# Attention scores as 64-column fp32 products in their own half of the PSUM partitions

## The chip, the core and the metric

The kernel runs on one core of a Trainium2 chip. The time is device time in microseconds (us) of one execution, given as a median of runs. TensorE (PE in the profile) multiplies a stationary operand, the weights, with a moving operand and writes to PSUM. VectorE is DVE, ScalarE is ACT, GpSimd is POOL, and SyncE (SP) issues the transfers.

## The reference, cut to what matters

The input is q, k, v of shape (8 batches, 8 heads, 576, 64) and p of shape (8, 8, 32, 64). Two attention steps come first, then two layers of products that do not matter for this change.

```python
def sm_attn(qq, kk, vv):
    s = scale * np.matmul(qq, kk.transpose(0, 1, 3, 2))
    s = s - np.max(s, axis=-1, keepdims=True)
    a = np.exp(s)
    a = a / (np.sum(a, axis=-1, keepdims=True) + 1e-09)
    return np.matmul(a, vv)
p_packed = sm_attn(p, k, v)               # 32 queries per head against 576 keys
out = sm_attn(q, p_packed, p_packed)      # 576 queries per head against 32 keys
...
h = max(x @ w1, x @ w2, x @ w3); x = h @ w_out        # 512 -> 768 -> 512
h = x @ w_in; x = (h * cos(h)) @ w_out                # 512 -> 2048 -> 512
```

## The kernel before

**Units.** The attention work is cut into 16 units, one for each batch `b` and each group `g` of four heads (two head pairs). A raw tile holds one head pair: 128 partitions are the 64 dimensions of two heads, 576 columns are the positions. A unit has two such tiles of k and two of q.

**The two score products of a unit.** `S1` multiplies the packed queries p with k, and `S2` multiplies the packed keys that step one has produced with q. Both call `scores(w, x)` (line 491; the matmul is at line 495). The weights `w` have shape 128 x 2 x 128: for each head pair `pi` there are 128 weight columns. Only 64 of them are filled, 32 for each of the two heads of the pair; the other 64 are zeros, cleared once at the start. In `pz` (step one) pair 0 fills columns 0 to 63 and pair 1 fills columns 64 to 127 (`pdst`, line 437). In `bt` (step two) it is the same for even batches, and the other way round for odd ones (`Ba`, line 608). The moving operand is one half `hf` of the 576 columns, 288 wide. For each half the two pairs are added up in one PSUM region of 128 partitions x 288 (`start` on the first, `stop` on the second); the zeros make the sum a mere placing of each pair in its own 64 partitions. So a unit has two score products of four matmul calls each, 32 products in all. Both operands are plain fp32, and the trace has two weight loads and two matmul instructions for each such call; nearly all other matmuls of the kernel are split by hand into float32r parts with one instruction for each call.

**What reads the scores.** The tile `big` is a PSUM tile of two banks. After `S1` DVE takes the maximum (`S1m`, line 508) and ACT the exponentials (`E1`, line 523); then come transposes (`Tp`, line 535), the product with v (`Pp`, line 560, or line 702 for the first two batches) and the transpose `Bp` (line 602), from which ACT and DVE fill `bt` and `wt` (lines 610, 613, 616). After `S2` DVE transposes the scores in blocks (`S2t`, line 629).

**The order.** Each engine works through a list that is fixed when the program is built. For the first two and the last two batches a planner (`Order`) sorts the steps by the costs in its table (2.1 for `S1` and `S2`); for the others `att_pos` places them by hand between the products of the first layer: `zps` (line 739, folding weights), `h` (line 818) and `x` (line 848). The diff changes neither the table nor the places, so every engine has its steps in the same order. After the attention, from about 505 us on, the second layer follows (lines 1363, 1794, 1832), in which there are no score products.

**Row halves in the kernel before.** For the first two batches line 702 ends each product with v in a matmul whose operands have only 64 rows. The trace shows it as `64*128`, beside `128*128` for the rest.

## Time and profile before

| | us |
|---|---|
| median of 3 runs | 1352.8 (1352.47 to 1353.12) |
| profiled execution | 1350.07 |
| its span, first to last instruction | 1348.3 |
| PE busy | 1313.1 (97%) |
| DVE, ACT, POOL busy | 898.2, 713.7, 363.1 |
| mean granted clock of TensorE | 0.995 |

The span is what the trace covers, and the profiled execution's own time is 1.8 us above it. Busy times are unions of instructions, so they say how much of the span an engine had something under way. Matmuls are pipelined: a matmul's duration is longer than the distance from its start to the next one's start, and it is this distance that counts when many follow each other.

### The profile page before, as it was taken

The page shows a single profiled execution, that of the slowest core. Times are in us where ns is not written, and L with a number is a line of the kernel's source. Part 1 is how long each engine was busy: PE and PEld are TensorE (multiplying, and loading weights), DVE is VectorE, ACT ScalarE, POOL GpSimd, SP SyncE. Part 2 cuts the span into 40 slices and gives each one's busy share as a digit, 9 for nine tenths or more (in the row PEclk, how much of TensorE's full clock was granted, in tenths as well). Part 3 has the DMA queues.
Part 4 walks back from the last instruction along what each step waited for, and adds up shares of the span by engine and source line. Part 5 has one row for each costly group of instructions (what it writes and reads, how often), then busy time and mean ns, then how long its engine had stood idle before and what let it go on. Part 6 is the DMA issues. An engine that isn't in the chain of part 4 may idle for free.

```text
span 1348.3 us, 22165 instructions
## 1 busy us (share of the span) xinstructions
PE 1313.1 (97%) x8130; PEld 1187.2 (88%) x8130; DVE 898.2 (67%) x1511; ACT 713.7 (53%) x1413; POOL 363.1 (27%) x340
## 2 busy tenths in 40 slices
PE   7889999999999998999999999999999999999998
PEld 5679999899989998888888899999999999999997
DVE  6885565546554677898578797666666566665655
ACT  4564435142513245555355576657666666666754
POOL 7572113030303006772013023203232032420300
PEclk9899999999999999999999999999999999999999
DMA  9777468445844478657021475756657566575630
GB/s 341 235 217 205 158 177 232 147 160 166 227 152 163 122 232 317 233 162 279 1 94 63 156 235 164 239 182 199 217 175 245 174 210 206 184 237 179 217 128 32
DMA packets 108140, 251.54 MB, mean 187 GB/s; under 512 B 17408, under 2 KB 40960, under 8 KB 108032
## 3 DMA queue, kind: packets, MB, share of 16 engines
q1 hardware_dynamic: 108032, 250.13, 57.9%
q8 instruction: 64, 1.05, 0.3%
q14 instruction: 44, 0.36, 0.1%
HBM read 180.88 MB, written 52.43 MB: 173 GB/s over the span
## 4 chain that ended last, share of the span: by engine, by line
PE 87%; DVE 7%; DMA 2%; ACT 2%; issue 2%; SPq 0%; POOL 0%; ACTq 0%; DVEq 0%; POOLq 0%
PE po L1832 26%; PE g L1794 21%; PE h L818 12%; PE x L848 9%; PE g L1363 6%; PE big L495 4%; PE zps L739 3%; PE po L1468 3%; DMA zd<-zx 1%; DVE m L833 1%; PE big L560 1%; PE big L702 1%; PE big L535 1%; DVE pv L577 1%; DVE wm L1575 0%
## 5 line engine op out<-in xcount | busy, mean ns | idle before, releaser
L1832 PE MATMUL po<-w,gh 128*128 128x512 f32 x1560 | 392.6, 389 | 0.0
L1832 PEld LDWEIGHTS po<-w,gh 128*128 128x128 f32 x1560 | 277.3, 188 | 43.9
L1794 PEld LDWEIGHTS g<-xc,wr 128*128 128x128 f32 x2160 | 284.2, 189 | 16.3
L1794 PE MATMUL g<-xc,wr 128*128 128x256 f32 x2160 | 288.4, 281 | 0.0
L818 PE MATMUL h<-at,z 128*128 128x256 f32 (+1 forms) x1728 | 249.6, 300 | 6.0 <-DMA z<-zx 3.0
L818 PEld LDWEIGHTS h<-at,z 128*128 128x128 f32 x1728 | 234.1, 191 | 12.8 <-DVE m L833 4.4
L1316 POOL TENSOR_TENSOR xc<-xr,xc 128x256 fp32r<-128x256 f32 x95 | 90.9, 977 | 498.0 <-ACT xc L1312 475.2
L1402 ACT ACTIVATE y<-y 128x512 f32<-128x512 f32 x144 | 91.0, 632 | 151.6 <-DVE y L1398 151.6
L848 PE MATMUL x<-hh,w 128*128 128x320 f32 (+1 forms) x1152 | 159.4, 296 | 4.6 <-DVE hh L303 1.6
L848 PEld LDWEIGHTS x<-hh,w 128*128 128x128 f32 x1152 | 154.7, 188 | 8.6 <-DVE hh L303 2.4
L1426 DVE TENSOR_TENSOR gh<-y,gh 128x512 fp32r<-128x512 f32 x144 | 109.0, 757 | 51.0 <-ACT gh L1422 50.9
L1406 DVE TENSOR_TENSOR y<-y,hs 128x512 f32<-128x512 f32 x112 | 84.2, 752 | 74.3 <-ACT y L1402 74.1
L1817 DVE TENSOR_TENSOR hs<-mc,g 128x256 f32<-128x256 f32 x168 | 70.0, 418 | 71.9 <-PE g L1794 69.9
L1422 ACT CAST gh<-y 128x512 fp32r<-128x512 f32 x144 | 88.8, 617 | 32.5 <-DVE y L1406 32.4
L1392 DVE SCALAR_TENSOR_TENSOR y<-y 128x512 f32<-128x512 f32 x128 | 93.9, 734 | 16.8 <-ACT y L1384 16.3
L833 DVE TENSOR_TENSOR m<-m,h 128x576 f32<-128x576 f32 x96 | 72.2, 752 | 48.2 <-PE h L818 27.2
L320 POOL TENSOR_SCALAR w<-wraw 128x512 fp32r<-128x512 f32 x56 | 88.9, 1598 | 28.3 <-DMA wraw<-w_in 10.2
L1805 ACT COPY mc<-g 128x256 f32<-128x256 f32 x168 | 62.3, 371 | 58.0 <-PE g L1794 57.4
L1363 PE MATMUL g<-x,w 128*128 128x512 f32 x384 | 92.0, 389 | 0.0
L756 DVE TENSOR_TENSOR zx<-zps,zx 128x512 fp32r<-128x512 f32 (+1 forms) x80 | 50.5, 635 | 57.8 <-ACT zx L751 53.6
L1363 PEld LDWEIGHTS g<-x,w 128*128 128x128 f32 x384 | 72.0, 188 | 14.9
L751 ACT CAST zx<-zps 128x512 fp32r<-128x512 f32 (+1 forms) x80 | 43.2, 542 | 74.5 <-PE zps L739 28.9
(120 smaller groups left out, 1575.8 us busy)
## 6 DMA issues: line engine op xcount, KB each, us to landing
wr<-sd SPq DMA_DIRECT2D x152, 512.0 KB, 3.5
zd<-zx SPq DMA_DIRECT2D x64, 256.0 KB, 3.6
z<-zd SPq DMA_DIRECT2D x32, 512.0 KB, 4.6
z<-zx SPq DMA_DIRECT2D x56, 256.0 KB, 3.2
wr<-sd SPq DMA_DIRECT2D x56, 256.0 KB, 3.2
sd<-w SPq DMA_DIRECT2D x24, 512.0 KB, 3.4
wraw<-w_out SPq DMA_DIRECT2D x22, 512.0 KB, 4.6
wraw<-w SPq DMA_DIRECT2D x18, 512.0 KB, 6.4
```

The lines of the kernel that those rows point to most:

```text
L320: nc.gpsimd.tensor_scalar(out=w[:, 1, :], in0=hi32.bitcast(F32), scalar1=0.0, scalar2=None, op0=ALU.mult)
L818: nc.tensor.matmul(ps[:, T0 + c0:T0 + c0 + nt], zt[b, j, g][:, x, c:c + P], at[b, g][:, y, c0:c0 + nt], start=(n == 0), stop=(n == 3 * NG ...
L833: nc.vector.tensor_tensor(out=m, in0=m, in1=ps[:, T0:T0 + S], op=ALU.max)
L848: nc.tensor.matmul(ps[:, T0 + c0:T0 + c0 + nt], w[:, x, d * P:(d + 1) * P], hh[f][:, y, c0:c0 + nt], start=(n == 0), stop=(n == 3 * NF - 1),)
L1316: EITHER[eng].tensor_tensor(out=x[:, 1, kk, :], in0=x_part(t, *XSRC[i], kk), in1=x[:, 0, kk, :].bitcast(F32), op=ALU.subtract)
L1363: nc.tensor.matmul(ps, w[:, a, kc * P:(kc + 1) * P], x2[t, kc][:, b, :], start=(n == 0), stop=(n == 3 * KC - 1),)
L1392: nc.vector.scalar_tensor_tensor(out=y, in0=r, scalar=MAGIC, in1=y, op0=ALU.subtract, op1=ALU.subtract)
L1402: nc.scalar.activation(out=r, in_=y, func=AF.Sin, scale=TWO_PI if c < NF2 else -TWO_PI)
L1422: nc.scalar.copy(g[:, 0, :], gs[c])
L1426: nc.vector.tensor_tensor(out=g[:, 1, :], in0=gs.pop(c), in1=g[:, 0, :].bitcast(F32), op=ALU.subtract)
L1794: nc.tensor.matmul(ps, w[:, a, c:c + P], x[:, b, kk, :], start=(i < 3 and n == 0), stop=(n == 5), skip_group_check=True,)
L1832: nc.tensor.matmul(po[t][s], g[:, a, s * P:(s + 1) * P], w[:, b, :], start=(f == 0 and i == 0), stop=(f == NF2 - 1 and i == 2),)
```

## The change

`scores` no longer adds two products of 128 weight columns into 128 PSUM partitions. Each pair multiplies only its 64 filled weight columns and writes its own 64 partitions, each matmul call being a group of its own. `swap` says which half belongs to which pair; step two passes the parity of the batch. The number of calls stays four for each product, with the same 288 moving columns, in the same order: for each half `hf`, first pair 0 and then pair 1.

```diff
-            def scores(self, w, x):
+            def scores(self, w, x, swap=0):
                 ps = self.big()
                 for hf in range(2):
                     for pi in range(2):
+                        c = (pi ^ swap) * D
                         nc.tensor.matmul(
-                            ps[:, hf, :HS], w[:, pi, :], x[pi][:, hf * HS:(hf + 1) * HS], start=(pi == 0), stop=(pi == 1)
+                            ps[c:c + D, hf, :HS], w[:, pi, c:c + D], x[pi][:, hf * HS:(hf + 1) * HS], start=True, stop=True
                         )
                 return ps[:, :, :HS]
...
             def S2(self):
-                self.s2 = self.scores(self.bt, self.qr)
+                self.s2 = self.scores(self.bt, self.qr, self.b % 2)
```

## Rows read from the trace of the kernel before

**Rows 1.** The page: busy time of the engines, and the chain that ended last.
```profile
PE 1313.1 (97%) x8130; PEld 1187.2 (88%) x8130; DVE 898.2 (67%) x1511; ACT 713.7 (53%) x1413; POOL 363.1 (27%) x340
...
PE 87%; DVE 7%; DMA 2%; ACT 2%; issue 2%; SPq 0%; POOL 0%; ACTq 0%; DVEq 0%; POOLq 0%
```

**Rows 2.** Busy time by stretch, all instructions: PE, PEld, DVE, ACT, POOL, clock, DMA.
```profile
0.00:100.00 100.00, 81.13 (x396) 65.07 (x397) 81.52 (x146) 54.36 (x105) 66.57 (x69) 0.95 0.81 267
100.00:505.00 405.00, 398.76 (x2721) 374.26 (x2721) 231.61 (x410) 144.44 (x290) 74.54 (x70) 1.00 0.60 178
505.00:1349.00 844.00, 833.23 (x5016) 747.86 (x5015) 585.04 (x956) 514.90 (x1019) 221.98 (x201) 1.00 0.55 181
```

**Rows 3.** Busy time by stretch of line 495 alone: PE, PEld, clock, DMA.
```profile
0.00:100.00 100.00, 22.27 (x64) 14.64 (x64) 0.95 0.81 267
100.00:505.00 405.00, 51.20 (x192) 35.46 (x192) 1.00 0.60 178
```

**Rows 4.** The chain, 100 to 505 us and 0 to 100 us: line 495's pieces.
```profile
by line: PE h L818 32.4%; PE x L848 26.4%; PE big L495 11.0%; PE zps L739 9.2%; PE big L560 3.5%; DVE m L833 2.3%; DVE pv L577 1.7%; issue 1.6%; PE big L535 1.5%; DMA zd<-zx 1.3%; DVE ms L637 1.0%; DVE e L641 1.0%; ACT e L651 0.8%; DVE hh L
...
221.16 1.94 PE big L495 x8
...
6.50 4.19 PE big L495 x8
13.97 3.15 PE big L495 x8
35.81 1.95 PE big L495 x8
42.47 4.21 PE big L495 x8
```

**Rows 5.** Line 495: durations in ns, least, median, most.
```profile
L495 PE MATMUL big<-raw,pz x128: 403/406/849, 6.5 to 422.9; 128*128 128x288 f32 x128
L495 PEld LDWEIGHTS big<-raw,bt x128: 186/190/193, 24.3 to 500.4; 128*128 128x128 f32 x128
L495 PE MATMUL big<-raw,bt x128: 403/406/510, 24.3 to 500.7; 128*128 128x288 f32 x128
```

**Rows 6.** Timeline, 220.6 to 223.5 us, PE and its weight loads: start, us.
```profile
220.77 1.88 PEld L495 LDWEIGHTS big<-raw,pz 128*128 128x128 f32 x8
221.00 2.10 PE L495 MATMUL big<-raw,pz 128*128 128x288 f32 x8
```

**Rows 7.** Timeline of weight loads around the 64-row matmuls of line 702.
```profile
50.42 0.84 PEld L702 LDWEIGHTS big<-raw,at 128*128 128x128 f32 x4
...
57.48 1.59 PEld L702 LDWEIGHTS big<-raw,at 128*128 128x128 f32 x8 [1.06 <-DVE at L694]
59.40 0.29 PEld L702 LDWEIGHTS big<-raw,at 64*128 64x128 f32 x2 [0.33 <-issue]
60.03 0.53 PEld L739 LDWEIGHTS zps<-w,wt 128*128 128x128 f32 x3 [0.33 <-issue]
```

**Rows 8.** Timeline of PE, 0 to 75 us: first and later score products.
```profile
6.50 4.18 PE L495 MATMUL big<-raw,pz 128*128 128x288 f32 x8 [2.66 <-DMA pz<-pT]
12.64 1.33 PE L535 MATMUL big<-ident,e 128*128 128x128 f32 x5 [1.97 <-ACT e L523]
13.84 3.27 PE L495 MATMUL big<-raw,pz 128*128 128x288 f32 x8
...
35.65 2.10 PE L495 MATMUL big<-raw,pz 128*128 128x288 f32 x8
39.71 1.13 PE L535 MATMUL big<-ident,e 128*128 128x128 f32 x5 [1.96 <-ACT e L523]
42.47 4.21 PE L495 MATMUL big<-raw,pz 128*128 128x288 f32 x8 [1.63 <-DVE at L694]
```

**Rows 9.** Waits of PE, 100 to 505 us: us in total, times, longest.
```profile
PE big L495 <- DVE wt L616: 1.5, 4, 0.4
PE big L495 <- DVE at L549: 0.3, 1, 0.3
```

**Rows 10.** Timeline of PE, 100 to 505 us: a score product after such a wait.
```profile
240.81 2.21 PE L495 MATMUL big<-raw,bt 128*128 128x288 f32 x8 [0.38 <-DVE wt L616]
```

## Prediction

> **What bounds the kernel now.** I read the page first. PE has work under way for 97% of the span, and 87% of the chain that ended last is PE [rows 1]. Busy time alone says little of a pipelined engine, so the stretches come next. From 100 to 505 us PE is busy for 398.8 of 405 us, and DVE for 231.6, ACT for 144.4, with the DMA engines at 0.60 [rows 2]: there PE sets the pace. Before 100 us PE is busy for 81.1 of 100 and DVE for 81.5; nobody is full, and the end is set by a chain through several engines. After 505 us line 495 has no instruction, so the change can only shift that part as a whole.

> Where is line 495? It has 64 matmul instructions before 100 us and 192 after, so at eight to a product there are 8 products early and 24 in the stretch that PE bounds [rows 3]. The chain of 100 to 505 us has 11.0% of its time on line 495 [rows 4], which is 44.6 us; 24 products of 1.94 us would be 46.6, so nearly every microsecond of these products is on the path. Of the early eight the chain names four, together 13.5 us [rows 4].

> **What one product costs now.** Eight instructions cover 2.10 us [rows 6], the last of them 0.406 by its own duration [rows 5], so starts lie (2.10 - 0.41) / 7 = 0.242 us apart: a slot. Eight slots are 1.94 us, which is also the chain's piece [rows 4]. The weight loads cover 1.88 us and begin 0.23 us ahead of the matmuls [rows 6]: each is hidden behind the matmul before it. So cutting a load from 128 to 64 columns gains nothing by itself here; the slot is that of the 288 moving columns, and the diff leaves their number, and that of the instructions, as it is.

> **What the change can give.** What changes is that two pairs no longer use the same part of the array's columns, nor the same PSUM partitions. If matmuls on different halves may run at the same time, the order of issue decides how much. In order they are A, A, B, B, A, A, B, B (two fp32 instructions for each call). [...] Then the slots are: A; A with B; B with A; A with B; B. Five slots in place of eight, 1.21 us, a gain of 3 x 0.242 = 0.73 us. If halves do not overlap, the gain is nothing. No row of before has two halves side by side: the only narrow matmuls, those of 64 rows, come in pairs on the same half [rows 7]. These are the two bounds, 0 and 0.73. I take 0.73: the operands, weight cells and results of A and B are disjoint after the change, and what the rows show of this engine is that it does start work that has its own place ahead of time, as the loads do [rows 6].

> [...]

> **What it costs.** The price is that of entering and leaving the narrow form. Line 702 pays it before the change, with 64 rows in place of 64 columns. Loads in a run of 256-column fp32 matmuls are (0.84 - 0.19) / 3 = 0.217 apart, 0.19 being one load's own time [rows 7]. From the first 64-row load at 59.40 to the first load after, at 60.03, there is 0.63 us for two matmuls, of which 0.43 would be their slots: 0.20 us more [rows 7]. The way in is the same: eight loads from 57.48 to 59.40 are 1.92 us. The loads stand still for 0.33 us on either side [rows 7]. The 0.20 has two parts. The two 64-row loads cover 0.29 us, so the second starts 0.29 - 0.19 = 0.10 after the first: the first load is not hidden, 0.10. The other 0.10 is the array running empty. A product surrounded by full-width work pays on both sides: on leaving 0.20, since the next load has 128 columns; on entering 0.10 of emptying and a load of 64 columns, between 0.05 (half of the 128-column load, an estimate) and 0.10. I take 0.15. Together 0.35, up to 0.40.

> [...]

> Between the halves there are three places where a load for the other half may come too late to be hidden, if loads are taken only one ahead of the matmuls. The bounds for that are 0 and 3 x 0.10 = 0.31 us; with loads half as long 0.16. Nothing of before shows loads more than one ahead, and nothing excludes it; I take 0.08, the middle of 0 and 0.16.

> **The sum.** From 100 to 505 us: 0.73 - 0.35 - 0.08 = 0.30 us for each of 24 products, 7.2 us. Five of them follow an idle PE, of 0.30 to 0.38 us [rows 9, 10]. The emptying falls into that wait, and the load after it stood bare before too (2.21 us against 2.10 [rows 10, 6]) and gets shorter. So entering changes these five from a cost of 0.15 to a gain of 0.05: 5 x 0.2 = 1.0 us more. The wait itself is for ACT and DVE work on a transpose that PE has just done, and moves with PE. Behind a product in PE's queue stand `h`, `zps` or `x`, which have their operands: the waits of PE on line 495 are 1.8 us of the 405 [rows 9]. So I count these 8.2 us in full.

> Before 100 us the products on the chain are four [rows 4, 8]. At 6.50 and 42.47 the slot is about 0.48, twice the other ((4.21 - 0.85) / 7, the longest record taken off [rows 5, 8]): 3 x 0.48 = 1.4 us each. Both follow a wait, so entering is free; the first also ends in a wait of 1.97, the other pays 0.2 for leaving. At 13.84 the mean slot is 0.41: 1.2 less 0.4 for both sides. At 35.65 it is 0.73 less 0.15, with a wait of 1.96 behind it. That makes 1.4 + 1.2 + 0.8 + 0.6 = 4.0. DVE is as busy as PE here, and DVE and DMA hold the chain between these pieces, so something else will end some of these waits: between 0 and 4.0, I take half, 2.0.

> Total: 8.2 + 2.0 = 10.2 us. The profiled execution would go from 1350.07 to about 1339.9. The median of the runs is 2.7 us above the profiled execution, and I forecast on that scale: 1352.8 - 10.2 = 1342.6. No change of order takes part in it. After 505 us, the transfers and waits hang on what PE finishes, and shift with it.

> **The rivals.**

> *The halves run one after the other.* Then the product keeps its eight slots and pays for the two switches: 24 x 0.40 = 9.6, less 1.0 for the five that come out of a wait, and 4 x 0.2 = 0.8 in the early chain (two sides at 13.84, one each at 35.65 and 42.47): +9.4 us, 1362.2. It speaks for it that slots are all that rows 6 show, that the number of columns streamed stays, and that a price of 0.20 is in the rows while the gain is not. Against it stands only that nothing is shared any more. It decides as soon as fewer than half of the three double slots appear: one of them, 0.24, does not pay the 0.35. I give it 24%.

> *The halves overlap, but each load for the other half stands bare.* With loads of 0.10 the product is 1.21 + 0.31 + 0.40 = 1.92 us, as before. The 24 products gain 0.5, the five waits 1.0, the early ones hardly anything: about 1.5 us, 1351.3. For it speaks that each load now begins with the matmul before it [rows 6] and never earlier. Against it: loads of half the columns should be shorter, and between two halves nothing has to be freed. I give it 12%.

> [...]

> *The gain is there, but the path moves off PE.* It would need PE to be short of work in 100 to 505 us, where it waits for little [rows 9]. This only trims the forecast's own size, and is in its range.

> **How the numbers follow.** About 0.2%, 2.7 us, is what a measurement of this kernel can tell from no change. The forecast case has 64%. Its best is 24 x (0.73 - 0.35) + 1.0 + 4.0 = 14.1 us, its least, with 0.16 for bare loads and no early gain, 24 x 0.22 + 1.0 = 6.3; so its own range is 1338.5 to 1348. The second rival has 12% and ends at 1351.3; the first, with 24%, lies at 1360 (switches of 0.35: 8.4 - 1.0 + 0.8 = 8.2) to 1362.5. Up to 1351.3 there are 76 in 100 at most, so the range has to reach to the lower end of the serial case: 1338.5 to 1361.5. Faster by over 0.2%: 0.64. Within 0.2%: 0.12. Slower: 0.24.

> **What the profile after would show.** Line 495 with weight loads of 64 columns, shorter than 190 ns, and eight matmuls whose starts come in five steps of 0.24, with pairs a few ns apart; a product in steady work that takes about 1.6 us from its first start to the next line's; the weight loads standing still for about 0.33 us ahead of it and behind it, as at line 702. Serial halves would show eight steps of 0.24. Bare loads would show steps of 0.29 to 0.35 where the half changes. The 505 us mark would come about 10 us earlier, and the rest would keep its length. I am wrong if the overlap is missing, or if the way in and out costs more for columns than for rows: at 0.33 us a side nothing is left of a product's gain.

## The result, and the profile after

The changed kernel takes 1337.8 us (median of 4 runs, 1335.6 to 1338.6) against 1352.6 for the kernel before: a ratio of 0.989, 95% interval 0.987 to 0.990, which is 13 to 17 us less. The prediction had the direction, but 10.2 us of gain and a lower end of 1338.5; the time lies 0.7 us below that end.

The page of the changed kernel, busy time of the engines and the chain, beside [rows 1]:

```profile
PE 1293.7 (97%) x8130; PEld 1154.9 (87%) x8130; DVE 897.1 (67%) x1511; ACT 713.5 (53%) x1413; POOL 361.5 (27%) x340
...
PE 85%; DVE 5%; DMA 5%; issue 1%; ACT 1%; SPq 1%; POOL 0%; ACTq 0%; DVEq 0%
```

The number of matmuls is the same, and so is PE's share of the span: PE still bounds the kernel, with 19.4 us less to do. Line 495 is now line 496. Its summary, durations in ns, beside [rows 5]:

```profile
L496 PEld LDWEIGHTS big<-raw,bt x128: 132/137/232, 25.1 to 487.4; 128*64 128x64 f32 x128
L496 PE MATMUL big<-raw,bt x128: 405/407/742, 25.1 to 487.7; 128*64 128x288 f32 x128
```

A weight load is shorter (137 ns for 190), a single matmul is as long as it was. So whatever the product gains does not come from narrower matmuls being faster. The timeline of PE and its loads shows where it comes from. The product is the one of [rows 6], with its neighbours:

```profile
216.22 0.85 PE L740 MATMUL zps<-w,wt 128*128 128x512 f32 x3
...
217.00 0.68 PEld L496 LDWEIGHTS big<-raw,pz 128*64 128x64 f32 x8 [0.36 <-DVE m L834]
217.00 1.19 PE L496 MATMUL big<-raw,pz 128*64 128x288 f32 x8
...
218.12 1.00 PEld L819 LDWEIGHTS h<-at,z 128*128 128x128 f32 x8 [0.44 <-issue]
```

Eight matmuls that took 2.10 us take 1.19. Less the last one's 0.41 and 0.05 for the first load, which now stands bare (0.29 us lie between the first start and the second step, 0.24 between the others), that is 0.73 us for three steps of 0.24. The same product cut into those steps (matmuls under way in each stretch, in brackets after the first time):

```profile
217.00:217.28 0.28, 0.28 (x2) 0.20 (x4) 1.00 0.66 161
217.28:217.52 0.24, 0.24 (x4) 0.14 (x2) 1.00 1.08 222
217.52:217.77 0.25, 0.25 (x4) 0.14 (x2) 1.00 1.11 229
217.77:218.01 0.24, 0.24 (x4) 0.00 (x0) 1.00 1.18 222
```

Two matmuls are under way from the first step on, and in each later one two more start while the last two drain. There are four slots with two matmuls each, not five with one, two, two, two, one. Nothing is exposed between them: the loads stand still only ahead of the product (0.36 us) and behind it (0.44).

Where the 14.5 us between the two profiled executions lie can be read from the start of the same instruction in both. The products at 100.53 and 448.01 us of the kernel before:

```profile
100.53 2.11 PE L495 MATMUL big<-raw,bt 128*128 128x288 f32 x8
...
448.01 2.10 PE L495 MATMUL big<-raw,bt 128*128 128x288 f32 x8
```

and the same two in the changed kernel, with the next one after the first:

```profile
99.81 1.19 PE L496 MATMUL big<-raw,bt 128*64 128x288 f32 x8
115.75 1.19 PE L496 MATMUL big<-raw,pz 128*64 128x288 f32 x8
...
434.71 1.19 PE L496 MATMUL big<-raw,bt 128*64 128x288 f32 x8
```

Up to the first of them 0.7 us were won, between them 12.6, and from there to the end of the spans (1348.3 and 1333.8) another 1.2.

### The profile page after: what moved, and what is told of

Same layout as the page of the kernel before. It is cut to its first block, busy times and chain, and to the rows that moved or that the text cites. A ratio compares the mean times of both kernels' runs of the same rounds, so it can differ in the third digit from the quotient of the medians.

```text
span 1333.8 us, 22171 instructions
## 1 busy us (share of the span) xinstructions
PE 1293.7 (97%) x8130; PEld 1154.9 (87%) x8130; DVE 897.1 (67%) x1511; ACT 713.5 (53%) x1413; POOL 361.5 (27%) x340
## 4 chain that ended last, share of the span: by engine, by line
PE 85%; DVE 5%; DMA 5%; issue 1%; ACT 1%; SPq 1%; POOL 0%; ACTq 0%; DVEq 0%
PE po L1833 27%; PE g L1795 21%; PE h L819 11%; PE x L849 11%; PE g L1364 6%; PE zps L740 3%; PE po L1469 3%; PE big L496 2%; DMA wraw<-w 1%; PE big L561 1%; DMA z<-zd 1%; DMA raw<-v 1%; DMA zd<-zx 1%; DVE m L834 1%; DMA z<-zx 1%
## 5 line engine op out<-in xcount | busy, mean ns | idle before, releaser
L1393 DVE SCALAR_TENSOR_TENSOR y<-y 128x512 f32<-128x512 f32 x128 | 93.9, 733 | 16.8 <-ACT y L1385 16.4
```

What stands on the lines that cost most here:

```text
L1393: nc.vector.scalar_tensor_tensor(out=y, in0=r, scalar=MAGIC, in1=y, op0=ALU.subtract, op1=ALU.subtract)
```

## The experiments

After the result there were three questions. Why four slots: does the engine take work out of order, or do neighbouring calls pair up in some other way? Is the price of a switch a fixed one, as the sum assumed? And what became of the early products?

**1. Calls of one pair next to each other** (`e1_order`). Only the order of the calls differs.

```diff
-                for hf in range(2):
-                    for pi in range(2):
+                for pi in range(2):
+                    for hf in range(2):
```

> The changed kernel with the four calls of a product in another order: both column halves of the moving operand for one pair, then both for the other. Each pair's calls are now neighbours. My theory (narrow matmuls are issued nearly in the order of the calls, and only neighbours on different halves of the array run together): overlap only where the first pair ends and the second begins, six to seven slots of 0.24 us, against four in the changed kernel; each product 0.5 to 0.73 us longer, the 24 products of the PE-bound stretch 12 to 17 us, total 1350 to 1355 us, about as before the change. Rival (the engine takes any narrow matmul whose half is free, whatever stands ahead of it in the queue): four slots again, same time as the changed kernel, 1338 us.

Measured: 1335.6 us, 0.988 of the kernel before (0.986 to 0.989). My theory was wrong and the rival right. PE and its loads, around the same product:

```profile
218.04 1.20 PE L496 MATMUL big<-raw,pz 128*64 128x288 f32 x8
...
218.04 0.69 PEld L496 LDWEIGHTS big<-raw,pz 128*64 128x64 f32 x8 [0.36 <-DVE m L834]
```

Eight matmuls in 1.20 us are four slots again, although four instructions of one half now stand ahead of the first of the other. An engine that kept to the order of the calls would need seven. The program built from this kernel does hold them in that order in all 32 products, four instructions of one half and then four of the other; so it is the engine that leaves it.

**2. How far it looks** (`e8_reach`). The first pair's two calls are issued three times, with the same values each time.

```diff
+                for pi in range(2):
+                    c = (pi ^ swap) * D
+                    for hf in (0, 1) if pi else (0, 1, 0, 1, 0, 1):
+                        nc.tensor.matmul(
+                            ps[c:c + D, hf, :HS], w[:, pi, c:c + D], x[pi][:, hf * HS:(hf + 1) * HS], start=True, stop=True
+                        )
```

> The calls in the order of the first experiment, but the two calls of the first pair are issued three times (the same values each time), so that twelve matmuls of one half stand ahead of the first of the other half. Theory of a long reach (any narrow matmul in the queue whose half is free starts): the other half's first matmul starts within 0.1 us of the first, twelve slots in all, 2.9 us a product. Theory of a short reach (it looks past about four matmuls): the other half starts only when eight or so of the first are done, still twelve slots. Strictly in order: it starts after eleven slots, fifteen slots in all, 3.6 us.

Measured: 1383.95 us in a single run. One product, all sixteen matmuls, and then the number under way in two stretches of it:

```profile
155.06 3.18 PE L496 MATMUL big<-raw,pz 128*64 128x288 f32 x16
```

```profile
155.00:157.00 2.00, 1.94 (x8) 1.15 (x9) 1.00 0.82 207
157.00:158.30 1.30, 1.24 (x9) 0.58 (x7) 1.00 0.99 332
```

3.18 us are twelve slots, 12 x 0.242 less the last slot plus its 0.41 and the bare loads. In the first 1.94 us eight matmuls started, one for each slot, so the other half stood idle. These slots are 0.24 us long although the matmuls are narrow: with one half alone nothing is gained. The remaining eight came in the last four slots, two at a time. The second half began within 7 ns of the ninth matmul of the first, when three more of the first were waiting, and it did so in all 32 products of this trace. The short reach is right: past three waiting matmuls, in these queues. That is just enough for the first experiment's order, and more than the change needs, where one waits.

**3. Half of each product narrow** (`e2_half`). The second half of the columns as before the change.

```diff
+                        if hf == 1:
+                            nc.tensor.matmul(
+                                ps[:, hf, :HS], w[:, pi, :], x[pi][:, hf * HS:(hf + 1) * HS], start=(pi == 0), stop=(pi == 1)
+                            )
+                            continue
                         c = (pi ^ swap) * D
```

> Only the first half of the moving columns as narrow products, the second half with 128 weight columns and zeros as before the change. My theory (a fixed price of about 0.34 us for entering and leaving the narrow form, and a gain of two slots, 0.48 us, for each half of the columns): each product gains 0.14 us against before, 24 of them 3.4 us, total about 1349 us. Rival (what is gained goes with the number of narrow calls, and switching costs next to nothing): half of the whole gain, about 1345 us.

Measured: 1345.4 us, 0.996 (0.994 to 0.997): 4 to 8 us less, with my 3.4 just outside and the rival's 7 inside. The total does not decide, since the early products and the runs' own spread are in it. The place does. Timeline of PE around one product, narrow part at line 501, wide part at line 496:

```profile
219.54 0.71 PE L501 MATMUL big<-raw,pz 128*64 128x288 f32 x4
220.18 1.24 PE L496 MATMUL big<-raw,pz 128*128 128x288 f32 x4
221.04 1.97 PE L824 MATMUL h<-at,z 128*128 128x256 f32 x12
```

The narrow part needs two slots, 0.48; then comes the way out, and four wide slots. From one full-width stream to the next the kernel before is later by 0.13 to 0.15 us for this product and 15 more of the 24 late ones (matched instructions in the two traces), as the fixed price says: 2 x 0.242 - 0.34. With the price in proportion it would be 0.31. So the price is fixed. The seven that follow a wait of PE, and the one at 100.38 us, gain 0.31 to 0.35, which my 3.4 left out; with them the late products come to 4.9 us, and the two profiles differ by 5.0.

**4. A tiny narrow matmul in the kernel before** (`e6_switch`). It writes 16 columns of PSUM that nothing reads.

```diff
                 for hf in range(2):
+                    if hf == 1:
+                        nc.tensor.matmul(ps[:D, 1, HS:HS + 16], w[:, 0, :D], x[0][:, :16], start=True, stop=True)
```

> The kernel before the change with one tiny narrow matmul (64 weight columns, 16 moving columns, into PSUM columns that nobody reads) between the two halves of each score product. My theory (entering and leaving the narrow form costs 0.14 and 0.20 us whatever the work): 0.35 to 0.45 us for each product, 8 to 11 us for the 24 of the PE-bound stretch, 1361 to 1364 us. Rival (the price is hidden when the work is small): the two passes alone, under 0.1 us for each product, 1354 us.

Measured: 1365.8 us, 1.010 (1.008 to 1.013), 10 to 17 us more, against 8 to 11. PE around one product:

```profile
227.81 1.13 PE L497 MATMUL big<-raw,pz 128*128 128x288 f32 x4
228.88 0.29 PE L495 MATMUL big<-raw,pz 128*64 128x16 f32 x2
229.09 1.24 PE L497 MATMUL big<-raw,pz 128*128 128x288 f32 x4
```

Each late product but one (0.06 at 104.89 us) grew by 0.40 to 0.44 us, the 24 together by 9.6; the rest of the 15 us of this profile is mainly before 100 us (4.4) and in one wait near 480 us (2.1 instead of 0.4 at that product). For two matmuls of 16 columns nearly all of the 0.42 is the way in and out. The rival, a hidden price, is refuted.

**5. Only the 24 late products** (`e3_late`) **and 6. only the eight early ones** (`e4_early`). Both have one condition in `scores`, `self.b < 2` or `self.b >= 2`, under which the calls of the kernel before are made.

```diff
+                        if self.b < 2:      # e4_early: self.b >= 2
+                            nc.tensor.matmul(
+                                ps[:, hf, :HS], w[:, pi, :], x[pi][:, hf * HS:(hf + 1) * HS], start=(pi == 0), stop=(pi == 1)
+                            )
+                            continue
```

> Narrow products only for the units of batches 2 to 7 (24 products), the eight products of batches 0 and 1 as before the change. My theory (the gain lies in the stretch that PE bounds; in the first 100 us the granted clock falls and takes back what the shorter products give): 14 us less than before, 1338 to 1339 us, the same as the changed kernel within 2 us, and a granted clock before 100 us as before the change (0.86 from 25 to 50 us, not 0.80). Rival (the early products are worth their 4 us of the chain): 1342 us.

> The other way round: narrow products only for the units of batches 0 and 1, the 24 others as before the change. My theory: 0 to 2 us less than before, 1351 to 1353 us, with a lower granted clock from 25 to 50 us (0.80 against 0.86). Rival (the early products are worth their 4 us of the chain): 1349 us.

Measured: the late ones alone 1336.2 us, 0.989 (0.987 to 0.990); the early ones alone 1350.3, 0.9985 (0.997 to 1.000), so 0.1 to 3.8 us less. The gain lies in the late products, as expected: the rival's 1342 us is outside the interval of the first. Its 1349 us is inside that of the second, so what the early products are worth is left open. What I said of the clock does not hold. Busy time and granted clock (third number from the end) before 100 us, first of the late-only kernel, whose early code is that of before:

```profile
25.00:50.00 25.00, 18.95 (x71) 14.12 (x70) 21.11 (x38) 10.91 (x22) 14.08 (x13) 0.80 1.00 348
...
75.00:100.00 25.00, 21.09 (x127) 18.47 (x128) 23.95 (x41) 17.25 (x34) 19.49 (x16) 0.86 0.80 227
```

and of the early-only kernel, whose early code is that of the change:

```profile
25.00:50.00 25.00, 18.64 (x87) 12.13 (x86) 23.16 (x45) 12.73 (x23) 16.72 (x14) 0.86 1.01 355
...
75.00:100.00 25.00, 21.66 (x143) 18.84 (x144) 24.40 (x41) 17.07 (x34) 16.33 (x12) 1.00 0.68 196
```

The wide early products have the lower clock here, 0.80 and 0.86, the narrow ones 0.86 and 1.00. And the changed kernel differs from itself, first in the profile of the result, then in that of `a2_again`:

```profile
25.00:50.00 25.00, 18.22 (x83) 11.51 (x83) 23.41 (x44) 13.05 (x25) 13.98 (x13) 0.80 1.03 357
```

```profile
25.00:50.00 25.00, 17.08 (x87) 11.26 (x86) 23.86 (x45) 13.27 (x25) 15.75 (x14) 0.86 1.03 364
```

The clock of the first 100 us differs from one execution to another, whichever form the products have.

**7. The changed kernel again** (`a2_again`) **and 8. the product with v in the same form** (`e5_pv`). The second is the changed kernel with one more edit, for batches 0 and 1:

```diff
-                    nc.tensor.matmul(
-                        ps[:, :2 * P],
-                        self.at[:rows, c * P:(c + 1) * P],
-                        r[:rows, o:o + 2 * P],
+                    for pi in range(2):
+                        nc.tensor.matmul(
+                            ps[pi * D:pi * D + D, pi * P:(pi + 1) * P],
+                            self.at[:rows, c * P + pi * D:c * P + pi * D + D],
+                            r[:rows, o + pi * P:o + (pi + 1) * P],
...
```

> The changed kernel once more, unaltered, on the chip of the three other runs of this group. From the first comparison: ratio 0.989 to before, within 0.987 to 0.990. If executions differ by the granted clock before 100 us, its runs spread over some 3 us.

> The changed kernel, and with it the product with v of batches 0 and 1 (line 702 before the change) in the same narrow form: 64 weight columns for each head pair, each pair with its own 128 columns of v in place of all 256. My theory (halves run together, a slot goes with the moving columns): ten slots of 0.215 us become ten double slots of about 0.11, each of the four products 0.8 to 1.0 us shorter after the price of the switch; three of the four lie on the chain before 100 us, so 2 to 3 us less than the changed kernel. Rival (the chain before 100 us is ended by DVE and DMA, and PE work cut there is not seen): the same as the changed kernel within 1 us.

Measured on one chip: the changed kernel 1335.4 us (1333.3 to 1336.2, about the spread expected), 0.988 (0.985 to 0.990), with the product 1334.35, 0.987 (0.985 to 0.989). The 1 us between them is not resolved. One such product in the changed kernel, and then in this one:

```profile
57.43 2.62 PE L703 MATMUL big<-raw,at 128*128 128x256 f32 x10 [0.64 <-DVE at L695]
```

```profile
52.59 1.46 PE L704 MATMUL big<-raw,at 128*64 128x128 f32 x20 [0.63 <-DVE at L695]
```

It is 1.16 us shorter, more than the 0.8 to 1.0 expected, but the time does not show it. The first product behind these, in the changed kernel again, then in this one and in the early-only kernel:

```profile
99.09 1.19 PE L496 MATMUL big<-raw,bt 128*64 128x288 f32 x8
```

```profile
95.29 1.19 PE L496 MATMUL big<-raw,bt 128*64 128x288 f32 x8
```

```profile
96.15 1.19 PE L501 MATMUL big<-raw,bt 128*64 128x288 f32 x8
```

This kernel comes there 3.8 us sooner than the changed kernel, and 1.3 us of that are left at the end of the two spans (1331.7 and 1333.0). So the rival's reason is not what these profiles show: the lead is there at 100 us and shrinks later. But the early-only kernel comes there nearly as soon without this edit, so one profile of each does not tell the edit from the spread between executions. The chain does not decide it either. The first pieces of the chain of this kernel are transfers:

```profile
5.53 7.43 DMA raw<-kT
15.02 5.99 DMA wraw<-w
21.03 9.44 DMA raw<-kT
```

In the changed kernel again, line 703 has 11.5% of the chain before 100 us. Which of the two expectations is right stays open. It is the fastest kernel of the study by its median, but not by a difference that can be told from none.

## Why the prediction was off, point by point

**What bounds the kernel: right.** The stretch that PE bounds gave nearly all of the gain, and experiment 3's and 5's late products moved the end by most of what they saved.

**The slots: wrong, and this is the step that failed.** The five slots that the prediction counts for the order A, A, B, B, A, A, B, B hold only if no matmul starts ahead of an earlier one. That was an assumption of mine, and no run shows it. The trace has four slots, and experiment 1 shows why: the first B is started beside the first A although a second A, and in the experiment two more, wait ahead of it. The 0.73 us that I gave as an upper bound was therefore no bound; the gain of slots is 4 x 0.242 = 0.97. With it the range's lower end was too high, too.

**The loads: also off, by less.** I took 0.08 us for loads that come too late between the halves. There are none of these in the steps, so the term is 0. The first rival's serial halves and the second rival's bare loads are both absent.

**The switches: right.** The first narrow matmul starts 0.32 us after the last `zps` in the profile above, whose slot is 0.233, and its bare load costs 0.05 more: late by 0.14 us in all (forecast 0.15). Behind the product the second full matmul starts 0.56 us after the last narrow one, against 0.36 after the last wide one in the kernel before: 0.20 (forecast 0.20). On both sides the first load of the next form starts 0.07 us ahead of the modelled end of the last matmul (217.00 against 217.07, 218.12 against 218.19), as at line 702 in the kernel before (59.40 against 59.47): that is what the prediction calls the array running empty. Experiments 3 and 4 have the same price in other surroundings: 0.34 out of the 0.48 that half a product saves, and 0.42 with two tiny matmuls in it.

What the prediction gave as 0.30 us for a product in full work is then 0.97 - 0.14 - 0.20 = 0.63. In matched instructions of the two traces 15 steady products show 0.61 to 0.65. After a wait it forecast 0.50 and the traces show 0.80 to 0.84; seven products behave so, not five, since the two that had 2.21 us without a long wait belong to them as well. One of them in the changed kernel, beside [rows 10]:

```profile
236.36 1.19 PE L496 MATMUL big<-raw,bt 128*64 128x288 f32 x8 [0.38 <-DVE wt L617]
```

The wait of 0.38 us is unchanged, as forecast: it moves with PE.

**Counting the PE-bound stretch in full: nearly right.** 17 x 0.63 + 7 x 0.81 would be 16.4 us, and it came to 13.8 with the tail. What is missing went mainly into new waits of PE. Behind the products at 99.81 and 115.75 the next line finds its operands not ready:

```profile
101.60 0.98 PE L740 MATMUL zps<-w,wt 128*128 128x512 f32 x3 [0.60 <-DVE zx L757]
...
117.27 0.96 PE L740 MATMUL zps<-w,wt 128*128 128x512 f32 x3 [0.32 <-DVE zx L757]
...
468.40 1.47 PE L819 MATMUL h<-at,z 128*128 128x256 f32 x9 [1.25 <-DMA z<-zx]
473.31 1.85 PE L819 MATMUL h<-at,z 128*128 128x256 f32 x12 [1.16 <-DVE m L834]
```

The first two take half and more of these products' gains (0.3 and 0.2 us are left by the matched instructions). The other two, near 470 us, take back more than one product's: by the matched instructions the changed kernel is 14.0 us ahead at 475 us of the kernel before, 11.2 at 510, and again 13.8 at 540, since the kernel before waits there, too.

**The early products: 2.0 forecast, 0.1 to 3.8 in experiment 6's timing.** By the start of the first late product the gain is 0.7 us in the profiles of before and after, 1.4 in the changed kernel again, and 4.4 in the early-only kernel. The term is neither confirmed nor refuted. How much of the 4.0 on PE's side other engines hide in each execution stays open, because the clock and the chain of that stretch differ between executions by more than the effect.

The sum with the terms as measured is 13.8 us for the late products and what follows them, and 0.7 before, 14.5 in all, which is what the two profiled executions differ by, against 8.2 and 2.0 in the prediction. The error is 24 x (0.24 + 0.08) = 7.7 us of slots and loads and 0.4 for the two further products after a wait, less 2.5 for what went into waits and 1.3 early, as these two profiles have it. So the losses that the prediction left out hid a part of its error. Two of its ends are also rounded: its own case adds up to 1338.7 to 1346.5, not 1338.5 to 1348, and the serial case with switches of 0.35 to 1361.0, not 1360; the measured time is below all of them.

A version in which the halves are narrow but cannot overlap was not tried, so the serial price (+9.4 us) was never measured as such; its parts were: the switch in experiment 4, and a slot of 0.24 us for a narrow matmul without a partner in experiment 2.

## What to carry to other kernels

If the weight columns of an fp32 product are half zeros, so that two products only place their results in different partitions, issue them as narrow products into their own partitions: here the two ran side by side in half the slots. The price was a fixed one here, 0.34 us for one way in and one way out of the narrow form, so put all narrow calls of a place together, and do not do it for less than about two slots of 0.24 us saved: two slots left 0.13 to 0.15 us of gain in experiment 3. For a forecast, an upper bound that rests on the order of issue has to be marked as resting on it: rows that show an engine busy one instruction at a time don't show that it must keep to their order.

## What the runs showed of the hardware that was not expected

In the first 100 us the granted clock differs from execution to execution, for the same code and in both directions: from 25 to 50 us its mean was 0.86 in the kernel before and 0.80 in the late-only kernel, which has the same products there, and 0.80 and 0.86 in two executions of the changed kernel. It also changes within that stretch of one execution: in the changed kernel a product takes 1.19 us at 37.86, at a granted clock of 1.00, and another, behind a wait of 1.99 us, 2.19 us at 43.78, at 0.50. Differences of a few us in that stretch are not to be explained from one profile of each kernel.
